# Attention with a gated convolution on one core: start addresses of the tiles that TensorE reads, and the layout of mirrored blocks

## The chip, the cores and the metric

The kernel runs on one core of a Trainium2 chip. The metric is the time of one execution on the device in microseconds (us); the median of several runs is given with the lowest and the highest.

## The reference

Eight batches of a sequence of 3200 with 256 channels. Attention weights are the squared positive part of the scaled products of z with itself, without a softmax; its result, times u, goes through a causal convolution of width 5 whose sigmoid gates a product with w_val, and a last product with w_out gives the output.

```python
scores = (1.0 / S) * np.matmul(z, z.transpose(0, 2, 1))    # z: (8, 3200, 64)
attn = np.maximum(scores, 0.0) ** 2
x = u * np.matmul(attn, v)                                  # u, v: (8, 3200, 256)
xp = np.concatenate([zeros((B, 4, D)), x], axis=1)
gate_pre = sum(conv_w[k] * xp[:, k:k + S, :] for k in range(5))
gate = 1.0 / (1.0 + np.exp(-gate_pre))
out = (gate * (x @ w_val)) @ w_out
```

## The kernel before

A batch's 3200 positions are 25 tiles of 128. As queries they are taken in seven chunks, four of 512 columns and then three of 384 (in the last batch five of 512, one of 384 and one of 256). As keys they are taken in 13 pairs of tiles, of which the last has one. A step is one chunk with one pair of key tiles; 8 x 7 x 13 = 728 steps follow one another in an order written out by hand.

All products are of float32 values cut into a high and a low part (type float32r), so one product is three on TensorE: low by high, high by low, high by high. In a step, `attend` or `attend_whole` multiplies the values of the key pair (`v_hl0` to `v_hl12`, the stationary operand, one tile for each pair) with the attention weights (`ah`, `al`, the moving operand, four buffers each) and adds them up in two PSUM banks (`acc0`, `acc1`): 2 key tiles x 3 parts x 2 halves of the channels = 12 products. The attention weights of the step three further on are made meanwhile: either from scores (z tiles `zhl0` to `zhl6`, one for each chunk, are stationary and moving operand; `scores`, then two activations on ACT, lines 399 and 400), or, since attention is symmetric, from a block that an earlier chunk has made, turned round on DVE (line 355) and kept in DRAM: a mirrored step. `weights_of` casts either kind to `ah` (line 402 on ACT, or 404 on DVE) and subtracts for `al` (line 405, DVE). A mirrored block comes from DRAM into `m` with the quarter a (32 keys of each tile) outermost and the key tile j inside it; `ah` and `al` have the same layout, and `attend_list` reads each key tile's part in four runs.

Two forms of step follow from this. Where the step three further on needs scores, whose products use 64 of the 128 rows, all products are issued as pairs of 64-row halves by `side_by_side` (line 292): 12 pairs for the values and 3 for the scores. This is a halved step. Where it is mirrored there are no scores, and `attend_whole` issues 12 products of 128 rows (line 440): a full step. From the second batch on, mirrored are 2, 4, 6, 8, 9 and 11 of the 13 steps in the second to seventh chunk.

Between the steps, a list with due times (`BEHIND`) lets the chunk before go through `gated` (times u, into `x`), the convolution on DVE (line 511), the sigmoid, `value` (with `w_val`, lines 292 and 548), `gate_value` (into `gv`, then `gvh` and `gvl`) and `project` (with `w_out`, moving operand; `gvh` and `gvl` stationary; lines 292 and 614).

SBUF tiles come from two pools. A tile with a tag of its own gets its own place, one behind the other in an order that the kernel's first uses give; tiles with a common tag and `bufs=1` share one. In the program's map of addresses, `cw_raw` (80 bytes for each partition, in a slot of 96) lies at 131264 and `x` (2 x 516 x 4 = 4128 bytes) at 217376; most other tiles have 2048, 3072 or 4096 bytes. The tiles that TensorE reads begin, modulo 512: the weights, `zhl0` to `zhl2`, `v_hl0` to `v_hl2`, `ah`, `al`, `xh`, `xl` at 192, all below 131072; `v_hl3` to `v_hl12`, `zhl3` to `zhl6` and `gvh` at 288, all above it; `gvl` at 320, also above. `cw_raw` is filled at step -1 (`fetch_conv`) and read until step 9 (`convert_conv`); `gv` is first written at step 19.

Of the kernel before, what the change touches and what calls it, by code (L numbers as in the profile page):

```python
# [7 lines left out]
F32 = mybir.dt.float32  # L8
F32R = mybir.dt.float32r
U32 = mybir.dt.uint32  # L10
AF = mybir.ActivationFunctionType
ALU = mybir.AluOpType
P = 128
BLK = 32
# [3 lines left out]
def attn_glu_kernel(  # L18
# [30 lines left out]
    KW = conv_w.shape[0]  # L49
    HALO = KW - 1  # L50
    NT = S // P
    DH = D // P
# [8 lines left out]
    i = even.index(base) if extra < n_chunks else None  # L61
# [5 lines left out]
    all_homes = [[(c, t) for c, n in enumerate(sz) for t in range(n)] for sz in all_sizes]  # L67
    CW = P * max(max(sz) for sz in all_sizes)

    const = ctx.enter_context(tc.tile_pool(name="const", bufs=1))  # L70
    sb = ctx.enter_context(tc.tile_pool(name="sb", bufs=2))
    ps = ctx.enter_context(tc.tile_pool(name="ps", bufs=2, space=bass.MemoryType.PSUM))
# [2 lines left out]
    def f32(ap):  # L75
        return ap.bitcast(F32)
# [42 lines left out]
    w_raw = {}  # L119

    def fetch_conv():
        w_raw["conv"] = sb.tile([P, DH, KW, 2], U32, name="cw_raw", bufs=1)
        for h in range(DH):
            nc.sync.dma_start(w_raw["conv"][:, h], conv_w[:, h * P : (h + 1) * P, :].rearrange("k p two -> p k two"))

# [210 lines left out]
    mirror, m_in, turned_, to_keep = {}, {}, {}, []  # L336

    def keeps(b, c):
        return b > 0 or c > 1

    def mirrored(b, c, i):
        return all(all_homes[b][t][0] < c and keeps(b, all_homes[b][t][0]) for t in range(pairs[i][0], sum(pairs[i])))

    def turn(b, c, i, a):

        w = all_sizes[b][c] * P
        if not keeps(b, c):
            return
        for j, g, t, m in runs(b, i):
            if g > c:  # L350
                size = all_sizes[b][g]
                if (b, c, g) not in turned_:
                    turned_[b, c, g] = sb.tile([P, 4 * CW], F32, name="turned", bufs=2)
                into = turned_[b, c, g][:, : w * size].rearrange("p (m t x) -> p t m x", t=size, x=BLK)
                nc.vector.transpose(  # L355
                    into[:, t : t + m], a[:, j * w : (j + m) * w].rearrange("p (t m x) -> p t m x", t=m, x=BLK)
                )
                if t + m == size:
                    to_keep.append((b, c, g))
# [22 lines left out]
    def cast_on_scalar(b, c, i):  # L382

        return mirrored(b, c, i) or (c == 0 and i > 2) or (c > 0 and (b == B - 1 or c < n_chunks - 1 or i < 4))

    def weights_of(b, c, i):

        k, n = pairs[i]
        w = all_sizes[b][c] * P
        ah = sb.tile([P, 2 * CW], F32R, name="ah", bufs=AHEAD + 1)  # L390
        al = sb.tile([P, 2 * CW], F32R, name="al", bufs=AHEAD + 1)
        hi, lo = ah[:, : n * w], al[:, : n * w]
        if mirrored(b, c, i):
            a = m_in.pop((b, c, i))[:, : n * w]
        else:
            s = st_.pop((b, c, i))
            a = sb.tile([P, 2 * CW], F32, name="a", bufs=2)[:, : n * w]
            each = n * w // 2
            nc.scalar.activation(a.rearrange("p (j x) -> p j x", j=2), s[:, :, :each], AF.Relu, scale=scale)  # L399
            nc.scalar.activation(a, a, AF.Square)  # L400
        if cast_on_scalar(b, c, i):
            nc.scalar.copy(hi, a)  # L402
        else:
            nc.vector.tensor_copy(hi, a)
        nc.vector.tensor_tensor(lo, a, f32(hi), op=ALU.subtract)  # L405
        if not mirrored(b, c, i):
            turn(b, c, i, a)
        at[b, c, i] = (ah, al)
# [4 lines left out]
    def attend_list(b, c, i, h, first=False, last=False):  # L413
        k, n = pairs[i]
        w = all_sizes[b][c] * P
        if (b, c) not in accs:
            accs[b, c] = [ps.tile([P, 512], F32, name=f"acc{x}", bufs=1) for x in range(DH)]
        ah, al = (x[:, : n * w] for x in at[b, c, i])
        if mirrored(b, c, i):
            ah, al = (x.rearrange("p (a j x) -> p j a x", a=P // BLK, j=n) for x in (ah, al))  # L420
        else:
            ah, al = (x.rearrange("p (j x) -> p j x", j=n) for x in (ah, al))
        vh, vl = vt[b, i][:, 0], vt[b, i][:, 1]
        acc = accs[b, c][h][:, :w]
        hs = slice(h * P, (h + 1) * P)
        out_ = []
        for j in range(n):
            for m, (vp, ap_) in enumerate(((vl, ah), (vh, al), (vh, ah))):
                out_.append((acc, vp[:, j, hs], ap_[:, j], first and j == m == 0, last and j == n - 1 and m == 2))
        return out_  # L430

    def attend(b, c, i, part):

        x = (i + part) % 2
        sides = (attend_list(b, c, i, h, part == 0 and i == 0, part == 1 and i == NP - 1) for h in (x, 1 - x))
        turn_round("acc", sides, part)

    def attend_whole(b, c, i, h):
        for out_, st, mv, first, last in attend_list(b, c, i, h, i == 0, i == NP - 1):
            nc.tensor.matmul(out_, st, mv, start=first, stop=last)  # L440
# [22 lines left out]
    xs, xhl, gates, gvs, pvs, pos = {}, {}, {}, {}, {}, {}  # L463

    def gated(b, c, h):
        w = all_sizes[b][c] * P
        if h == 0:
            xs[b, c] = sb.tile([P, DH, HALO + CW], F32, name="x", bufs=1)
        x = xs[b, c]
        nc.vector.tensor_tensor(  # L470
            x[:, h, HALO : HALO + w], accs[b, c][h][:, :w], ut[b, c][:, h, :w], op=ALU.mult
        )
        if h == 0:
            if c == 0:
                nc.gpsimd.memset(x[:, :, :HALO], 0.0)
            else:
                nc.gpsimd.tensor_copy(x[:, :, :HALO], halos.pop((b, c - 1)))
# [201 lines left out]
    for b in range(B):  # L679
# [34 lines left out]
        else:  # L714
# [14 lines left out]
            for load in loads:  # L729
                at_step(*load)  # L730
    at_step(-1, fetch_conv)
    at_step(4, fetch_weights, "val", w_val, "gvh")
    at_step(9, fetch_weights, "out", w_out, "ob")
# [4 lines left out]
    with tc.manual_schedule():  # L738
        for s in range(min(todo), N):
            b, c, i = steps[s] if s >= 0 else (0, 0, -1)  # L740
# [3 lines left out]
            if s <= END:  # L744
# [25 lines left out]
                if i == NP - 1:  # L770
                    for h in range(DH):
                        gated(b, c, h)
# [3 lines left out]
                if ahead:  # L776
                    weights_of(*ahead)
            elif s == END + 1:
                for h in range(DH):
                    for r in range(s, N):  # L780
                        attend_whole(*steps[r], h)
                    gated(b, c, h)
                    x_high(b, c, one[h])
                    x_low(b, c, one[h])
                    for k in range(KW):
                        conv(b, c, h, k)
                    sigmoid(b, c, one[h])
# [47 lines left out]
```

## Time and profile before

| | |
|---|---|
| median of 3 runs | 2372.27 us (2371.66 to 2373.46) |
| the profiled execution | 2374.35 us, its span 2372.6 us |
| TensorE products busy | 2349.4 us, 99% of the span, 18894 of them |
| TensorE weight loads busy | 2065.3 us, 87% |
| VectorE (DVE) busy | 1792.8 us, 76% |
| ScalarE (ACT) busy | 1776.0 us, 75% |

Busy is the time in which an engine has at least one instruction under way. Products of TensorE overlap: the next starts while the last columns of one drain, so a product's own duration is longer than its share of the time. In a stretch that TensorE fills without a gap, the elapsed time divided by the number of products is the distance from one start to the next. Stretches below begin where a step begins and end where one ends.

### The profile page before, as it was taken

How to read it: one execution, taken by the hardware profiler on the slowest of the kernel's cores; microseconds unless marked ns; L12 is line 12 of the kernel's file. 1: busy time of each engine (PE TensorE's matmuls, PEld its weight loads, DVE VectorE, ACT ScalarE, POOL GpSimd, SP SyncE). 2: the span in 40 equal slices, each digit the busy share in tenths (PEclk: the TensorE clock that was granted, in tenths of full speed). 3: DMA queues.
4: the chain of work that ended last, by engine and by line, in shares of the span. 5: the costliest groups of instructions: out<-in, count | busy, mean ns of one | idle time of the engine just before them, and what ended most of it. 6: DMA issues, size and time to landing. Idle time of an engine off the chain costs nothing.

```text
span 2372.6 us, 47211 instructions
## 1 busy us (share of the span) xinstructions
PE 2349.4 (99%) x18894; PEld 2065.3 (87%) x18894; DVE 1792.8 (76%) x2265; ACT 1776.0 (75%) x2313; POOL 33.6 (1%) x108
## 2 busy tenths in 40 slices
PE   8999999999999999999999999999999999999998
PEld 6898998889888899888988899888998889988888
DVE  7776777787777777778787787777877778677775
ACT  7888868777777767777688775887768876687764
POOL 0000000000000000000000000000000000000000
PEclk9999999999999999999999999999999999999999
DMA  6155597778977789667896778866897778966552
GB/s 128 37 141 138 147 237 182 206 189 212 244 185 198 186 224 242 179 185 197 238 227 165 192 213 233 213 180 178 230 231 190 181 200 236 250 144 156 162 170 76
DMA packets 660013, 446.12 MB, mean 188 GB/s; under 512 B 349008, under 2 KB 614480, under 8 KB 659792
## 3 DMA queue, kind: packets, MB, share of 16 engines
q1 hardware_dynamic: 658736, 442.97, 70.9%
q8 instruction: 148, 2.42, 0.4%
q14 instruction: 73, 0.60, 0.1%
q10 hardware_dynamic: 1056, 0.13, 0.0%
HBM read 240.92 MB, written 202.05 MB: 187 GB/s over the span
## 4 chain that ended last, share of the span: by engine, by line
PE 96%; ACT 2%; DVE 1%; DMA 1%; issue 0%; SPq 0%; ACTq 0%; DVEq 0%
PE acc L292 45%; PE acc L440 28%; PE s L292 11%; PE misc L292 6%; PE misc L614 4%; PE misc L548 1%; ACT a L400 0%; ACT a L399 0%; DMA z_raw<-in_z_dram 0%; ACT ah L402 0%; DMA u_raw<-in_u_dram 0%; DVE gate L511 0%; DVE al L405 0%; DMA m<-mir 0%; DVE x L470 0%
## 5 line engine op out<-in xcount | busy, mean ns | idle before, releaser
L292 PE MATMUL acc<-ah,v_hl 64*128 64x512 f32 (+1 forms) x6656 | 1114.7, 380 | 8.3 <-DVE x L470 3.5
L292 PEld LDWEIGHTS acc<-ah,v_hl 64*128 64x128 f32 x6656 | 663.4, 185 | 120.4 <-issue 14.5
L405 DVE TENSOR_TENSOR al<-a,ah 128x1024 fp32r<-128x1024 f32 (+3 forms) x429 | 472.2, 1101 | 380.5 <-ACT ah L402 375.4
L292 PE MATMUL acc<-al,v_hl 64*128 64x512 f32 (+1 forms) x3328 | 665.1, 378 | 0.0
L440 PE MATMUL acc<-ah,v_hl 128*128 128x384 f32 (+2 forms) x2272 | 644.2, 359 | 0.9 <-ACT ah L402 0.9
L399 ACT ACTIVATE a<-s 128x1024 f32<-128x1024 f32 (+3 forms) x429 | 397.1, 926 | 219.5 <-PE s L292 217.7
L440 PEld LDWEIGHTS acc<-ah,v_hl 128*128 128x128 f32 x2272 | 416.5, 188 | 50.8 <-issue 6.6
L400 ACT ACTIVATE a<-a 128x1024 f32<-128x1024 f32 (+3 forms) x429 | 413.4, 964 | 14.0
L440 PE MATMUL acc<-al,v_hl 128*128 128x384 f32 (+2 forms) x1136 | 404.9, 356 | 0.1
L405 DVE TENSOR_TENSOR al<-m,ah 128x768 fp32r<-128x768 f32 (+2 forms) x299 | 306.5, 1025 | 115.5 <-ACT ah L402 114.7
L402 ACT CAST ah<-a 128x1024 fp32r<-128x1024 f32 (+3 forms) x391 | 374.0, 957 | 12.7
L292 PEld LDWEIGHTS acc<-al,v_hl 64*128 64x128 f32 x3328 | 339.8, 185 | 46.2
L402 ACT CAST ah<-m 128x768 fp32r<-128x768 f32 (+2 forms) x299 | 262.5, 892 | 150.8 <-DMA m<-mir 106.3
L355 DVE STREAM_TRANSPOSE turned<-a 128x1024 f32<-128x1024 f32 (+3 forms) x314 | 314.9, 1010 | 1.8 <-DMA mir<-turned 1.7
L511 DVE SCALAR_TENSOR_TENSOR gate<-x,cw,gate 128x512 f32<-128x512 f32 (+2 forms) x448 | 304.8, 680 | 4.1
L292 PE MATMUL s<-zhl,zhl 64*128 64x512 f32 (+3 forms) x1950 | 275.3, 373 | 0.0
L440 PEld LDWEIGHTS acc<-al,v_hl 128*128 128x128 f32 x1136 | 213.7, 188 | 16.7 <-DVE al L405 0.3
L292 PEld LDWEIGHTS s<-zhl,zhl 64*128 64x128 f32 x1950 | 194.4, 186 | 29.5 <-ACT a L399 0.6
L564 ACT CAST gvh<-gv 128x512 fp32r<-128x512 f32 (+2 forms) x112 | 64.3, 574 | 58.1 <-DVE gv L560 58.1
L292 PE MATMUL s<-zhl 64*128 64x512 f32 (+3 forms) x624 | 91.3, 376 | 7.1 <-DVE zhl L203 7.1
L516 ACT ACTIVATE gate<-gate 128x512 f32<-128x512 f32 (+2 forms) x112 | 65.3, 583 | 39.2 <-DVE gate L511 39.2
L492 ACT CAST xh<-x 128x1024 fp32r<-128x1024 f32 (+2 forms) x57 | 53.7, 942 | 42.8 <-DVE x L470 42.7
(97 smaller groups left out, 1861.0 us busy)
## 6 DMA issues: line engine op xcount, KB each, us to landing
m<-mir SPq DMA_DIRECT2D x187, 384.0 KB, 5.0
mir<-turned SPq DMA_DIRECT2D x332, 192.0 KB, 3.9
mir<-turned SPq DMA_DIRECT2D x188, 256.0 KB, 4.1
m<-mir SPq DMA_DIRECT2D x94, 512.0 KB, 6.1
v_hl<-v_kept SPq DMA_DIRECT2D x84, 512.0 KB, 7.0
v_kept<-v_made SPq DMA_DIRECT2D x71, 512.0 KB, 4.0
u_raw<-in_u_dram SPq DMA_DIRECT2D x264, 64.0 KB, 3.3
out_dram<-ob SPq DMA_DIRECT2D x33, 512.0 KB, 4.1
```

Of the source, the lines that this page charges most:

```text
L292: ins = nc.tensor.matmul(out_, st[r], mv[r], start=first, stop=last)
L355: nc.vector.transpose(into[:, t : t + m], a[:, j * w : (j + m) * w].rearrange("p (t m x) -> p t m x", t=m, x=BLK))
L399: nc.scalar.activation(a.rearrange("p (j x) -> p j x", j=2), s[:, :, :each], AF.Relu, scale=scale)
L400: nc.scalar.activation(a, a, AF.Square)
L402: nc.scalar.copy(hi, a)
L405: nc.vector.tensor_tensor(lo, a, f32(hi), op=ALU.subtract)
L440: nc.tensor.matmul(out_, st, mv, start=first, stop=last)
L492: nc.scalar.copy(xhl[b, c][0][:, hs, :w], xs[b, c][:, hs, HALO : HALO + w])
L511: nc.vector.scalar_tensor_tensor(g, tap, cw[:, h, k : k + 1], g, op0=ALU.mult, op1=ALU.add)
L516: nc.scalar.activation(g, g, AF.Sigmoid)
L564: nc.scalar.copy(gvs[b, c][0][:, e, :w], gv_[b, c, e][:, :w])
L614: nc.tensor.matmul(out_, st, mv, start=first, stop=last)
```

## The change

One constant is added: `X_ROW`, the row of `x`, is 512 + 64 elements instead of 516, so `x` has 4608 bytes. `cw_raw` gets the tag of `gv`, so it takes that tile's place instead of one of its own. With these two, all tiles that TensorE reads begin at 192 modulo 512. In `weights_of`, a mirrored block is still read from `m` with the quarter outermost, but `ah` and `al` are written with the key tile outermost and the quarter inside it; `attend_list` then reads every block as it reads one that was made from scores.

```diff
@@ -67,6 +67,9 @@
     CW = P * max(max(sz) for sz in all_sizes)
 
+    X_ROW = CW + P // 2
+    assert HALO <= P // 2
+
     const = ctx.enter_context(tc.tile_pool(name="const", bufs=1))
@@ -119,7 +122,7 @@
     def fetch_conv():
-        w_raw["conv"] = sb.tile([P, DH, KW, 2], U32, name="cw_raw", bufs=1)
+        w_raw["conv"] = sb.tile([P, DH, KW, 2], U32, name="cw_raw", tag="gv", bufs=1)
         for h in range(DH):
@@ -391,7 +394,8 @@
         hi, lo = ah[:, : n * w], al[:, : n * w]
         if mirrored(b, c, i):
-            a = m_in.pop((b, c, i))[:, : n * w]
+            a = m_in.pop((b, c, i))[:, : n * w].rearrange("p (a j x) -> p a j x", a=P // BLK, j=n)
+            hi, lo = (x.rearrange("p (j a x) -> p a j x", a=P // BLK, j=n) for x in (hi, lo))
         else:
@@ -416,10 +420,7 @@
         ah, al = (x[:, : n * w] for x in at[b, c, i])
-        if mirrored(b, c, i):
-            ah, al = (x.rearrange("p (a j x) -> p j a x", a=P // BLK, j=n) for x in (ah, al))
-        else:
-            ah, al = (x.rearrange("p (j x) -> p j x", j=n) for x in (ah, al))
+        ah, al = (x.rearrange("p (j x) -> p j x", j=n) for x in (ah, al))
@@ -465,7 +466,7 @@
         if h == 0:
-            xs[b, c] = sb.tile([P, DH, HALO + CW], F32, name="x", bufs=1)
+            xs[b, c] = sb.tile([P, DH, X_ROW], F32, name="x", bufs=1)
         x = xs[b, c]
```

## Rows read from the trace of the kernel before

**Rows 1.** The page: TensorE's busy time, and its granted clock in 40 slices.

```profile
PE 2349.4 (99%) x18894; PEld 2065.3 (87%) x18894; DVE 1792.8 (76%) x2265; ACT 1776.0 (75%) x2313; POOL 33.6 (1%) x108
...
PEclk9999999999999999999999999999999999999999
```

**Rows 2.** The page: the chain that ended last, shares of the span by engine.

```profile
PE 96%; ACT 2%; DVE 1%; DMA 1%; issue 0%; SPq 0%; ACTq 0%; DVEq 0%
```

**Rows 3.** TensorE's waits, costliest first: us in total, times, longest us.

```profile
PE s L292 <- DVE zhl L203: 7.1, 1, 7.1
PE acc L292 <- DVE x L470: 3.5, 2, 3.2
```

**Rows 4.** TensorE's products by shape: count, busy us, mean ns, idle us.

```profile
L292 PE MATMUL acc<-ah,v_hl 64*128 64x512 f32 x4936 | 866.5, 394 | 8.1 <-DVE x L470 3.5 <-DVE v_hl L250 2.6 <-ACT a L400 1.7
L292 PE MATMUL acc<-al,v_hl 64*128 64x512 f32 x2468 | 518.5, 394 | 0.0
L440 PE MATMUL acc<-ah,v_hl 128*128 128x384 f32 x1356 | 357.5, 340 | 0.0
L440 PE MATMUL acc<-ah,v_hl 128*128 128x512 f32 x832 | 270.9, 398 | 0.0
...
L440 PE MATMUL acc<-al,v_hl 128*128 128x512 f32 x416 | 164.0, 394 | 0.0
...
L614 PE MATMUL misc<-w_out_hi,gvl 128*128 128x256 f32 x260 | 74.1, 285 | 0.0
```

**Rows 5.** Windows, full steps of v_hl11, v_hl1 (512 columns): us, PE, PEld, clock, DMA.

```profile
1043.65:1046.46 2.81, 2.81 (x13) 2.26 (x12) 1.00 1.05 343
1053.44:1056.16 2.72, 2.72 (x13) 2.25 (x12) 1.00 1.16 269
```

**Rows 6.** Windows, halved steps: second chunk's v_hl2, v_hl3, v_hl4; fourth chunk's v_hl7.

```profile
963.26:966.71 3.45, 3.45 (x32) 1.00 0.01 2
966.71:970.23 3.52, 3.52 (x33) 1.00 0.75 173
970.23:973.75 3.52, 3.52 (x32) 1.00 0.21 41
1075.85:1079.36 3.51, 3.51 (x32) 1.00 0.18 74
```

**Rows 7.** Windows, 384 columns: full (runs, one run), value; halved (runs, one run).

```profile
1096.09:1104.55 8.46, 8.46 (x48) 8.46 (x49) 1.00 0.86 226
1124.93:1128.05 3.12, 3.12 (x19) 2.96 (x18) 1.00 0.93 286
...
1177.15:1179.24 2.09, 2.09 (x12) 1.93 (x12) 1.00 0.98 305
...
1114.94:1117.60 2.66, 2.66 (x32) 1.00 0.87 201
1117.60:1120.22 2.62, 2.62 (x32) 1.00 0.46 70
```

**Rows 8.** Windows, 256 columns: v_hl1 and v_hl2, v_hl3 and v_hl4; 24 projections.

```profile
2336.69:2339.57 2.88, 2.88 (x26) 2.88 (x25) 1.00 0.31 91
2339.57:2342.39 2.82, 2.82 (x26) 2.82 (x25) 1.00 0.86 284
...
1047.87:1050.70 2.83, 2.83 (x24) 2.79 (x23) 1.00 1.04 339
```

**Rows 9.** DVE by shape: count, busy us, mean ns, idle us and what ended it.

```profile
L405 DVE TENSOR_TENSOR al<-a,ah 128x1024 fp32r<-128x1024 f32 x302 | 369.8, 1225 | 266.5 <-ACT ah L402 261.9 <-PE s L292 2.4
L355 DVE STREAM_TRANSPOSE turned<-a 128x1024 f32<-128x1024 f32 x177 | 219.1, 1238 | 0.8 <-DMA mir<-turned 0.7
```

**Rows 10.** Windows, the fourth batch's fifth, sixth, seventh chunk: us, DVE busy, clock, DMA.

```profile
1096.09:1130.90 34.81, 27.16 (x37) 1.00 0.77 206
1130.90:1164.40 33.50, 24.37 (x38) 1.00 0.78 200
1164.40:1199.18 34.78, 26.89 (x41) 1.00 1.06 270
```

## The prediction

> **What bounds the kernel now.** I read the busy shares first, then the chain of work that ended last, then TensorE's waits, then TensorE's products by shape, and last the elapsed time of single steps. The reader is to see that TensorE is the only thing that counts: it is busy 99% of the span with its clock granted in full, that is at 2.4 GHz, in every slice [rows 1]; the chain runs through it for 96% [rows 2]; of its waits the costliest comes to 7.1 us in the whole span and the next to 3.5 us [rows 3]. So the time is the number of products times the distance from the start of one to the start of the next. That distance is what I look for, and not the mean duration, which holds the drain behind the last column as well.
>
> The distance is not a constant. A step takes the 12 products of one pair of key tiles (v_hl0 to v_hl12). At line 440, where a product uses all 128 rows, a step of v_hl11 with 512 columns takes 2.81 us, 234 ns for each product; a step of v_hl1, with the same shape, takes 2.72 us, 227 ns [rows 5]. Since 512 columns at 2.4 GHz are 213 ns, the bare overhead falls from 21 to 14 ns. In the steps where products run as pairs of 64-row halves beside the scores (line 292), 15 pairs with 512 columns take 3.45 us with v_hl2 and 3.52 us with v_hl3 and v_hl4 [rows 6]. The break lies between v_hl2 and v_hl3, and all later tiles are like v_hl3. In the program's map of addresses that is where cw_raw lies: 80 bytes in a slot of 96. Ahead of it every tile that TensorE reads begins at 192 modulo 512 (the weights, zhl0 to zhl2, v_hl0 to v_hl2, ah, al, xh, xl); behind it at 288 (v_hl3 to v_hl12, zhl3 to zhl6, gvh); gvl, behind x with its 4128 bytes, at 320. So it is the steps whose stationary tile and moving tile begin at different residues that are slow. A hint that the two count together: in the fourth chunk the scores read moving and stationary from tiles at 288, and there a halved step takes 3.51 us, with the key products still mixed [rows 6].
>
> A second loss is in mirrored steps, where the moving operand is read in four runs. With 384 columns, four full steps in runs take 8.46 us for 48 products, 176.3 ns each; one and a half steps read in one run take 3.12 us for 18, 173.3 ns [rows 7]. The first are of v_hl0 to v_hl3, on both sides of the break, the second of tiles at 288; twelve value products with weights at 192 and one run take 2.09 us, 174 ns [rows 7]. So at 384 columns it is the runs that cost and not the residue. Halved, a step of 2.66 us becomes one of 2.62 us [rows 7].
>
> **The change part by part.** Products are counted in the order of the program; the sum of the shapes is in [rows 4].
>
> 1. cw_raw shares gv's buffer and x grows to 4608 bytes, nine times 512. All other tiles there are multiples of 512 bytes, so everything TensorE reads comes to 192, the state that v_hl0 to v_hl2 have today.
>  - Full steps, 512 columns: 852 of the 1248 products of line 440 take a stationary tile at 288, which is 71 steps. 71 x (2.81 - 2.72) = 6.4 us saved.
>  - Halved steps, 512 columns: 5820 of the 7404 products take one at 288, which is 242.5 steps. Some 50 of them have scores from zhl3 and go from 3.51 to 3.45, the other 192 from 3.52 to 3.45: 50 x 0.06 + 192 x 0.07 = 16.4 us. The scores' own gain is in these steps. Least: 0.06 for all, 14.6 us. Most: if pairs come down to the 227 ns that a full product reaches, 15 x 0.227 = 3.40 us and 242 x 0.12 = 29 us. I take 3.45, for it is measured on the very form.
>  - 384 columns: nothing, by the 173.3 and 174 ns of [rows 7]. The value products of lines 292 and 548 read tiles at 192 already: nothing.
>  - 256 columns: here equal residues look worse. In the last chunk two steps with v_hl1 and v_hl2 take 2.88 us (120 ns), two with v_hl3 and v_hl4 2.82 us (117.5 ns) [rows 8]. The projection of line 614 now runs at 2.83/24 = 117.9 ns [rows 8]; if it goes to 120, its 780 products and the 276 pairs of line 292 lose 1056 x 2.1 = 2.2 us. The other end is nothing, since projection reads its weights as moving operand, which that row does not show. I take the loss.
>  - Other work: cw_raw is filled at step -1 and last read at step 9; gv is first written at step 19, so no wait arises. x, gv and halo are read by DVE, ACT and POOL alone; POOL's copies into x touch the same few columns.
>
> 2. Mirrored blocks are written by key tile, so their products read one run. With 384 columns 1536 full products are 128 steps: 128 x (8.46/4 - 3.12/1.5) = 128 x 0.035 = 4.5 us. 1584 halved ones are 66 steps: 66 x 0.04 = 2.6 us. With 512 columns runs cost nothing: the step of v_hl1 in [rows 5] is a mirrored one. The price is on ACT and DVE, whose cast (line 402) and subtraction (line 405) now put down 128 or 96 elements at a time instead of 1024 or 768 in one. The nearest row is DVE's transpose (line 355), which writes runs of 32 elements: 1238 ns against 1225 for a plain subtraction of the size [rows 9]. I take nothing to 13 ns for each of 299 blocks, and it is covered: in the fifth to seventh chunk of a batch DVE works 27.16 of 34.81, 24.37 of 33.50 and 26.89 of 34.78 us [rows 10]. No DMA, wait or queue is moved.
>
> Sum: 6.4 + 16.4 - 2.2 + 4.5 + 2.6 = 27.7 us. A faster TensorE asks more of ACT and DVE by 1%, which the same windows leave room for. The profiled execution took 2374.35 us (span 2372.6, 1.75 around it), the median of the runs is 2372.27; 2374.35 - 27.7 = 2346.7 and, from the median, 2344.6. I forecast 2345. With the bounds (14.6 or 29 for the halved steps, 0 or 2.2 for the 256 columns, runs at half or all) the forecast's own range is 2333 to 2350.
>
> **A rule against it.** The rows show that a tile's residue and a moving operand's runs go with 3 to 7 ns of a product [rows 5, 7]. The Trainium skill's page "SBUF — State Buffer", section Specifications (TRN2), gives lines of 16 bytes and full bandwidth from two hits on one; 192, 288 and 320 and runs of 384 bytes are all multiples of 16, so by it neither edit would change anything. Its page "TensorE: Matmul & The Clock Gate", Part 2, says that loading the next weights takes no read bandwidth from the running product, by which a stationary tile's place could not lengthen one. The trace differs by the 7 ns above, if these belong to the place and not to the step.
>
> **The rivals.**
> A: the residue is not what counts. v_hl0 to v_hl2 also lie below address 131072 and v_hl3 to v_hl12 above it, and ah and al below; the trace can't part this from the residue. Then the tiles stay where they are in that sense, and only part 2 remains: 2372.3 - 7.1 = 2365. Against it stands little: the fourth chunk's scores, both operands above, are no slower, so lying above is not slow in itself [rows 6]. Chance 0.12.
> B: the differences belong to the steps (what else runs in the first three of a chunk), and neither place nor runs matter: 2372. Against it: the break falls between v_hl2 and v_hl3 in chunks with quite different neighbours [rows 5, 6]. The 16-byte rule named above would end here. Chance 0.06.
> C, slower: writing in pieces is dear on DVE, and DVE becomes the bound of the late chunks. It has 7.65, 9.13 and 7.89 us free there [rows 10] for 8, 9 and 11 mirrored blocks. Up to some 1.0 us more for each, a doubling, the 27.7 us are not used up; at 1.2 us more the chunks run over by 2.0, 1.7 and 5.3 us, 9 us in each of seven batches, and 2345 + 63 = 2408. Against it stand the 13 ns of the transpose. Chance 0.04.
>
> **How the numbers follow.** Forecast 0.78, A 0.12, B 0.06, C 0.04. About 0.2% (4.7 us) is what a measurement here can tell from no change. Faster by more than that: all of the forecast and two thirds of A, 0.86; same: the rest of A and B, 0.10; slower 0.04. The range reaches from the forecast's lower end to A's time with a little room, 2333 to 2367, and leaves out B, C and what I have not thought of.
>
> **What will show it.** If part 1 is right, full steps of v_hl10 and v_hl11 take 2.72 us and halved steps 3.45 us whatever their tile; if A holds, they stay at 2.81 and 3.52. If part 2 is right, full mirrored steps of the fifth chunk take 2.08 us. The projection of 24 products tells by 2.83 or 2.88 us whether 256 columns lose. For C, lines 402 and 405 would show it in their means. I am wrong in size if halved steps fall below 3.40 us, and in kind if a step of v_hl11 doesn't move.

## The result, and the profile after the change

| | before | after |
|---|---|---|
| median (lowest to highest) | 2372.27 us (2371.66 to 2374.03), 5 runs | 2350.34 us (2346.95 to 2352.55), 5 runs |
| ratio to before, 95% interval | 1 | 0.9904 (0.989 to 0.9919) |
| the profiled execution, its span | 2374.35 us, 2372.6 us | 2350.68 us, 2348.9 us |

The kernel is 1.0% faster, 21.9 us by the medians and 23.7 us by the two profiled executions. The forecast was 2345 us with a range of 2333 to 2367. The direction and the mechanism came as forecast; the gain was put 4 us too high by the profiled executions and 5 to 6 us by the medians.

The page of the kernel after shows nearly the same shares as [rows 1]: TensorE is as full as before, its clock is granted in full (a 9 is 90% or more) in every slice, and it is busy for 23.6 us less.

```profile
PE 2325.8 (99%) x18894; PEld 2047.1 (87%) x18894; DVE 1790.1 (76%) x2265; ACT 1774.0 (76%) x2313; POOL 34.2 (1%) x108
...
PEclk9999999999999999999999999999999999999999
```

The next fence has windows of the trace after. A line gives the stretch, its length in us, TensorE's busy time with the number of products under way in it, in some lines the same for weight loads, then the granted clock, the share of DMA and GB/s. They are, in order, full steps with 512 columns of v_hl11, v_hl1 and v_hl10; a halved step of v_hl4 in the second chunk; halved steps with 384 columns in the fifth chunk, v_hl7, which is mirrored, and v_hl8, which is not; full steps with 384 columns of v_hl1 and v_hl10; and the 24 projections between the third and the fourth chunk.

```profile
1032.80:1035.52 2.72, 2.72 (x14) 2.25 (x13) 1.00 1.04 331
1042.50:1045.22 2.72, 2.72 (x14) 2.25 (x13) 1.00 1.09 334
1074.81:1077.68 2.87, 2.87 (x12) 2.36 (x13) 1.00 0.97 310
...
960.35:963.81 3.46, 3.46 (x32) 1.00 0.22 41
1103.31:1105.94 2.63, 2.63 (x32) 1.00 1.13 237
1105.94:1108.57 2.63, 2.63 (x32) 1.00 0.60 155
...
1086.72:1088.80 2.08, 2.08 (x13) 2.08 (x13) 1.00 0.71 115
1111.11:1113.33 2.22, 2.22 (x13) 2.22 (x13) 1.00 0.95 228
...
1036.88:1039.75 2.87, 2.87 (x26) 1.00 1.03 343
```

The step of v_hl11 went from 2.81 us [rows 5] to 2.72, what v_hl1 had and kept; the halved step from 3.52 [rows 6] to 3.46; the full mirrored step with 384 columns from 2.115 (a quarter of the 8.46 of [rows 7]) to 2.08; the halved mirrored v_hl7 from 2.66 to 2.63 and v_hl8 from 2.62 to 2.63 [rows 7]; the projection from 2.83 [rows 8] to 2.87. Two rows did not do as told: v_hl10 with 512 columns, for which the prediction had 2.72 us, only went from 2.91 to 2.87, and with 384 columns it became slower, from 2.18 to 2.22. The rows of before for these two:

```profile
1086.13:1089.04 2.91, 2.91 (x14) 1.00 0.95 324
1122.75:1124.93 2.18, 2.18 (x14) 1.00 0.95 231
```

ACT and DVE did not feel the writing in pieces. In the groups by shape of the trace after, the casts of mirrored blocks at line 406 and the subtractions at line 409 (402 and 405 before, with means of 832, 1047, 949 and 1222 ns there) have the means they had:

```profile
L406 ACT CAST ah<-m 128x768 fp32r<-128x768 f32 x194 | 159.1, 833 | 58.2 <-DMA m<-mir 36.2 <-PE acc L441 16.4 <-ACT ob L631 4.4
L406 ACT CAST ah<-m 128x1024 fp32r<-128x1024 f32 x94 | 96.7, 1049 | 80.4 <-DMA m<-mir 72.0 <-PE acc L441 8.2
...
L409 DVE TENSOR_TENSOR al<-m,ah 128x768 fp32r<-128x768 f32 x194 | 183.8, 947 | 40.6 <-ACT ah L406 39.6
L409 DVE TENSOR_TENSOR al<-m,ah 128x1024 fp32r<-128x1024 f32 x94 | 114.8, 1221 | 73.7 <-ACT ah L406 73.7
```

### The profile page after: what moved, and what is told of

Its sections match the earlier page's. It is cut to its first block, busy times and chain, and to the rows that moved or that the text cites. A ratio compares the mean times of both kernels' runs of the same rounds, so it can differ in the third digit from the quotient of the medians.

```text
span 2348.9 us, 47211 instructions
## 1 busy us (share of the span) xinstructions
PE 2325.8 (99%) x18894; PEld 2047.1 (87%) x18894; DVE 1790.1 (76%) x2265; ACT 1774.0 (76%) x2313; POOL 34.2 (1%) x108
## 4 chain that ended last, share of the span: by engine, by line
PE 94%; ACT 2%; DVE 1%; DMA 1%; issue 1%; SPq 0%; ACTq 0%; DVEq 0%
PE acc L295 44%; PE acc L441 28%; PE s L295 11%; PE misc L295 6%; PE misc L615 4%; PE misc L549 1%; ACT a L404 1%; ACT a L403 1%; DMA u_raw<-in_u_dram 1%; ACT ah L406 1%; DMA v_raw<-in_v_dram 0%; DMA z_raw<-in_z_dram 0%; DVE al L409 0%; DVE x L471 0%; DVE gate L512 0%
## 5 line engine op out<-in xcount | busy, mean ns | idle before, releaser
L295 PE MATMUL acc<-ah,v_hl 64*128 64x512 f32 (+1 forms) x6656 | 1103.3, 377 | 7.0 <-DVE v_hl L253 2.6
L295 PEld LDWEIGHTS acc<-ah,v_hl 64*128 64x128 f32 x6656 | 656.3, 185 | 118.6 <-issue 13.3
L295 PE MATMUL acc<-al,v_hl 64*128 64x512 f32 (+1 forms) x3328 | 658.3, 376 | 0.0
L441 PE MATMUL acc<-ah,v_hl 128*128 128x384 f32 (+2 forms) x2272 | 637.8, 356 | 0.8 <-ACT ah L406 0.8
```

The lines of the kernel that those rows point to most:

```text
L295: ins = nc.tensor.matmul(out_, st[r], mv[r], start=first, stop=last)
```

## The experiments

Each kernel is told as a diff or in words; lines left out of a diff are marked by three dots. Fences hold windows as above, all from the fourth batch. From the third to the seventh batch a step takes the same time in each batch to 10 ns, so steps can be compared to that accuracy, while the time of a run scatters by 2 us and more. In what follows the distance is the start of the stationary tile less the start of the moving one, in bytes, modulo 512.

### One part at a time

The addresses alone (e1), in the kernel before, with the constant `X_ROW` added as in the change:

```diff
-        w_raw["conv"] = sb.tile([P, DH, KW, 2], U32, name="cw_raw", bufs=1)
+        w_raw["conv"] = sb.tile([P, DH, KW, 2], U32, name="cw_raw", tag="gv", bufs=1)
...
-            xs[b, c] = sb.tile([P, DH, HALO + CW], F32, name="x", bufs=1)
+            xs[b, c] = sb.tile([P, DH, X_ROW], F32, name="x", bufs=1)
```

> Addresses alone: cw_raw in gv's place, x with 4608 bytes, mirrored blocks laid out as before. If the two parts add up, the steps with 512 columns take what they take after the change (full v_hl11 2.72 us, halved 3.46 us) and mirrored steps with 384 columns what they took before (2.11 us full, 2.66 us halved): 2350.3 + 6.3 = 2357 us. The 6.3 us are the difference of the steps with 384 columns between the two traces (4.2 full, 2.1 halved). If the runs cost only while the tiles are apart, 2350 us.

Measured: 2353.47 us, ratio 0.9921 (0.9904 to 0.9937). Windows: full v_hl11 and halved v_hl4 with 512 columns; full v_hl1 and halved v_hl7, both mirrored, with 384.

```profile
1032.97:1035.69 2.72, 2.72 (x13) 1.00 1.07 357
960.53:963.99 3.46, 3.46 (x34) 1.00 0.20 38
1086.93:1089.04 2.11, 2.11 (x13) 1.00 0.87 119
1103.66:1106.31 2.65, 2.65 (x32) 1.00 0.83 200
```

The steps with 512 columns have all of their gain, those with 384 remain in runs at 2.11. The time is 3.5 us lower than the expectation's sum, which took the whole difference of the two traces in these steps for the layout's. 1.3 us of it are a wait at the start of the second batch, of which more below. From the third to the seventh batch each one is 0.5 to 0.7 us slower than after the change, but the first two are no slower in sum, since their waits differ from trace to trace.

The layout alone (e2), in the kernel before: the edits in `weights_of` and `attend_list`, with cw_raw and x as they were.

> The layout of mirrored blocks alone: cw_raw and x as before. If the parts add up: mirrored steps with 384 columns at 2.08 us, steps with 512 columns as before (full v_hl11 2.81 us, halved 3.52 us): 2372.3 - 6.3 = 2366 us. If the layout is worth nothing by itself, 2372 us; if casts that write in pieces cost ACT or DVE something, lines 402 and 405 have other means than 1047 and 1222 ns.

Measured: 2366.25 us, ratio 0.9976 (0.9967 to 0.9985). Windows: the same four steps, and the halved v_hl8, which is not mirrored.

```profile
1040.45:1043.26 2.81, 2.81 (x13) 1.00 1.03 331
967.02:970.55 3.53, 3.53 (x32) 1.00 0.21 40
1094.97:1097.05 2.08, 2.08 (x13) 1.00 0.82 110
1111.54:1114.16 2.62, 2.62 (x32) 1.00 0.73 188
1114.16:1116.78 2.62, 2.62 (x32) 1.00 0.89 200
```

This is rival A's time, 2365, and the layout's share is as the prediction had it, with 2.08 and 2.62 us. But the halved steps take 2.62 us here, where tiles are 96 bytes apart, and 2.63 after the change, where they are not. So at 384 columns equal starts cost something in halved steps; one run gives a mirrored one 0.04 us at 96 bytes (2.66 [rows 7] to 2.62) and only 0.01 to 0.02 with equal starts (2.65 in e1 to 2.63 after); and the two parts don't quite add up: they gain 18.9 and 6.1 us alone, 25.0 in sum, and 21.9 together, with a scatter of the runs of 2 us.

### Is it the distance of the two starts, or the place of one?

Moving operands elsewhere (e8): in the kernel after, `v_made`, with the raw tile that shares its place, gets 96 bytes more and cw_raw a slot of 416 bytes. ah, al, v_hl1, v_hl2 and zhl2 then begin at 288, all else at 192.

```diff
-        w_raw["conv"] = sb.tile([P, DH, KW, 2], U32, name="cw_raw", tag="gv", bufs=1)
+        cw_raw = sb.tile([P, 104], U32, name="cw_raw", bufs=1)
+        w_raw["conv"] = cw_raw[:, : DH * KW * 2].rearrange("p (h k two) -> p h k two", h=DH, two=2)
...
-        v_made[b, g, t] = sb.tile([P, 2, 2, D], F32R, name="v_made", bufs=1)
+        v_made[b, g, t] = sb.tile([P, 4 * D + 24], F32R, name="v_made", bufs=1)[:, : 4 * D].rearrange("p (x t d) -> p x t d", x=2, t=2)
```

> As after the change, but ah, al, v_hl1, v_hl2 and zhl2 begin at 288 modulo 512, everything else that TensorE reads at 192. Theory (the distance counts): steps of v_hl1 and v_hl2 stay at 2.72 us with both operands at 288, steps of v_hl0 and v_hl3 to v_hl12, whose stationary tile is still at 192, go to 2.81 us full and 3.5 halved; time about 2365 us. Rival (the stationary tile's own residue counts, 192 fast and 288 slow): v_hl11 stays at 2.72 us, v_hl1 goes to 2.81, time about 2355 us.

Measured: 2373.93 us, ratio 1.0009 (1.0 to 1.0019). Windows: full steps of v_hl11, v_hl1 and v_hl2, then the halved v_hl4, all with 512 columns; full steps of v_hl3 and v_hl11 with 384.

```profile
1040.08:1042.88 2.80, 2.80 (x14) 1.00 1.01 334
1049.93:1052.70 2.77, 2.77 (x14) 1.00 1.11 275
1052.70:1055.51 2.81, 2.81 (x14) 1.00 0.78 147
966.52:970.02 3.50, 3.50 (x33) 1.00 0.19 39
...
1098.92:1101.04 2.12, 2.12 (x13) 1.00 1.06 393
1121.52:1123.64 2.12, 2.12 (x14) 1.00 0.79 238
```

v_hl11 lies where it is fast after the change, at 192, and is slow, because ah and al have moved away: the stationary tile's own place decides nothing. v_hl2 takes 2.81 us as it does before and after the change in this place, where the first halved products follow on it. v_hl1, with equal starts, takes 2.77 and not the 2.72 expected: it comes behind the slow v_hl0, and in the trace its products start 235 ns apart at first and 227 at the end, as those of v_hl10 do after the change. The whole is no faster than before and 9 us slower than the theory's 2365. The theory's figures are those of a distance of +96. At -96 one key pair more has unequal starts, and full steps with 384 columns take 2.12 us, where they take 2.08 at +96 (v_hl3 and v_hl11 in e2). So a distance of -96 undoes all that the two parts gain, and at 384 columns its sign counts.

All tiles elsewhere (e3): in the kernel after, the constant tile `cw` is made 96 bytes larger, so that everything behind it begins at 288.

```diff
-        cw = const.tile([P, DH, KW], F32, name="cw")
+        cw = const.tile([P, 40], F32, name="cw")[:, : DH * KW].rearrange("p (h k) -> p h k", k=KW)
```

> As after the change, but all tiles that TensorE reads begin at 288 modulo 512. Theory (the distance of the two starts counts, not where they lie): the same steps as after the change, 2.72 us for v_hl11 and 3.46 halved, 2350 us. Rival (192, or a start on a line of 64 bytes, is the good place): 2.80 us and more, 2365 us.

Measured: 2350.17 us, ratio 0.9909 (0.9892 to 0.9925); v_hl11, halved v_hl4, halved v_hl8 with 384 columns:

```profile
1034.54:1037.26 2.72, 2.72 (x13) 1.00 1.02 342
962.10:965.56 3.46, 3.46 (x33) 1.00 0.18 35
1107.69:1110.32 2.63, 2.63 (x32) 1.00 0.65 105
```

The steps are those of the kernel after. 192 is no better place than 288, and a start on a multiple of 64 bytes is not what counts; what the steps of e2, e3 and e8 with 512 columns go with is the distance.

### Which distances?

Four kernels differ from the kernel after in cw_raw's slot alone, n bytes (576, 544, 128, 256). The tiles behind it, v_hl3 to v_hl12, zhl3 to zhl6, gvh and gvl, then begin 64, 32, 128 and 256 bytes further than the others, modulo 512.

```diff
-        w_raw["conv"] = sb.tile([P, DH, KW, 2], U32, name="cw_raw", tag="gv", bufs=1)
+        cw_raw = sb.tile([P, n // 4], U32, name="cw_raw", bufs=1)
+        w_raw["conv"] = cw_raw[:, : DH * KW * 2].rearrange("p (h k two) -> p h k two", h=DH, two=2)
```

> As after the change, but v_hl3 to v_hl12, zhl3 to zhl6, gvh and gvl begin at 256 modulo 512, 64 bytes from the other tiles. Theory (the distance of stationary and moving start modulo 512 counts): full steps of v_hl11 at 2.81 us, halved at 3.5, time 2366 us, what the layout alone gives. Rival (what counts is that a tile begins on a line of 64 bytes, which 288 does not): 2.72, 3.46 and 2350 us.

> As after the change, but the later tiles begin 32 bytes further, at 224 modulo 512. If any distance costs, v_hl11 takes 2.80 us and the time is 2364 us, as 64 bytes apart; if the loss grows with the distance (64: 2.80, 96: 2.815), 2.75 to 2.79 us and some 2357 us.

> As after the change, but the later tiles begin 128 bytes further, at 320. If the loss grows with the distance, v_hl11 at 2.82 us or more and 2366 us; if the period is 128 bytes, 2.72 and 2350.

> As after the change, but the later tiles begin 256 bytes further, at 448. If the period is 256 bytes, v_hl11 at 2.72 us and 2350 us; if it is 512, half the period apart, 2.8 us and about 2365, or less than that if the loss has its peak near 96 bytes on either side.

| distance | median us, ratio (95% interval) | v_hl11, full | v_hl4, halved | v_hl8, halved, 384 columns |
|---|---|---|---|---|
| 0 (after) | 2350.34, 0.9904 (0.989 to 0.9919) | 2.72 | 3.46 | 2.63 |
| 32 | 2363.81, 0.9968 (0.9957 to 0.9979) | 2.80 | 3.52 | 2.61 |
| 64 | 2364.26, 0.9964 (0.9951 to 0.9977) | 2.80 | 3.50 | 2.64 |
| 96 (e2) | 2366.25, 0.9976 (0.9967 to 0.9985) | 2.81 | 3.53 | 2.62 |
| 128 | 2364.90, 0.9971 (0.9962 to 0.998) | 2.80 | 3.49 | 2.66 |
| 256 | 2348.75, 0.9905 (0.989 to 0.992) | 2.72 | 3.46 | 2.63 |

The windows of the kernel with 32 bytes, then of the one with 256, for the three steps of the table:

```profile
1037.23:1040.03 2.80, 2.80 (x13) 1.00 1.03 333
963.83:967.35 3.52, 3.52 (x33) 1.00 0.20 39
1110.86:1113.47 2.61, 2.61 (x32) 1.00 0.69 108
```

```profile
1031.01:1033.73 2.72, 2.72 (x14) 1.00 1.10 346
958.56:962.02 3.46, 3.46 (x32) 1.00 0.21 39
1104.15:1106.78 2.63, 2.63 (x32) 1.00 0.83 126
```

At 512 columns each distance from 32 to 128 bytes costs about the same, 0.08 to 0.09 us for a full step and 0.03 to 0.07 for a halved one; the expectation that the loss grows with the distance fell. 256 bytes are as good as none, and the -96 of e8, which is 160 modulo 256, is slow. So a period of 256 bytes fits all of them, and the 512 of the change were more than needed: its tiles would also do at 192 and 448. The rival of the lines of 64 bytes fell with the kernel at 64 (2.80 us), that of a period of 128 bytes with the one at 128.

At 384 columns the distance alone does not decide. With 64 bytes, full steps of v_hl3 and v_hl11 take, in this order:

```profile
1094.64:1096.76 2.12, 2.12 (x13) 1.00 1.05 396
1117.14:1119.22 2.08, 2.08 (x13) 1.00 0.92 264
```

### A version by width of the product

The prediction had put down that 256 columns are slower with equal starts, and e2 and e5 show the same of halved steps with 384. So the starts were set apart where the products are narrow, first for the projection (e9), by moving gvh's and gvl's data 64 bytes on. Their buffers are 512 bytes larger, and so is the raw weight that shares gvh's.

```diff
-                sb.tile([P, DH, CW], F32R, name="gvh", bufs=1),
-                sb.tile([P, DH, CW], F32R, name="gvl", bufs=1),
+                sb.tile([P, DH * CW + 128], F32R, name="gvh", bufs=1)[:, 16 : 16 + DH * CW].rearrange("p (h w) -> p h w", h=DH),
+                sb.tile([P, DH * CW + 128], F32R, name="gvl", bufs=1)[:, 16 : 16 + DH * CW].rearrange("p (h w) -> p h w", h=DH),
```

> As after the change, but the data of gvh and gvl begin 64 bytes further, at 256 modulo 512, while w_out stays at 192. Theory (products of 256 columns are slower where both operands start at one residue): the 24 projections of a chunk with 512 columns go back from 2.87 to 2.83 us or a little less, some 2 us over the kernel, 2348 us; no other step changes. Rival (the projection became slower for another reason, such as x's place): 2.87 and 2350 us.

Measured: 2348.79 us, ratio 0.9904 (0.9887 to 0.992). The 24 projections between third and fourth chunk:

```profile
1036.06:1038.89 2.83, 2.83 (x26) 1.00 0.89 267
```

They are back at 2.83 us with no other tile moved modulo 512, so it was the equal starts that had made them slower. The median is 1.5 us lower than that of the kernel after, but the kernel before was 1.8 us faster too in this round of runs (2370.5 us), and the ratio is the same: in the whole time no gain is shown.

Then the attention weights of the narrow chunks as well (e10): e9 with

```diff
+        o = 56 if w < CW else 0
-        hi, lo = ah[:, : n * w], al[:, : n * w]
+        hi, lo = ah[:, o : o + n * w], al[:, o : o + n * w]
...
-        at[b, c, i] = (ah, al)
+        at[b, c, i] = (ah[:, o : o + n * w], al[:, o : o + n * w])
```

> As e9, and in chunks narrower than 512 columns ah and al are written 224 bytes further into their buffers, so the stationary tile begins 32 bytes behind the moving one modulo 256. Theory: the distance that costs at 512 columns is worth something at 384: halved steps 2.633 to 2.613 us, the first full step of v_hl10 2.216 to 2.19, other full steps 2.08 as they are; 2 us less than e9, 2346 us. Rival (384 columns are best with equal starts, and what e2 showed came from elsewhere): 2348 us, halved steps at 2.633.

Measured: 2346.3 us (2345.74 to 2346.46), ratio 0.9894 (0.9879 to 0.9908). Halved v_hl8 and full v_hl10 with 384 columns; v_hl11 with 512:

```profile
1103.68:1106.30 2.62, 2.62 (x34) 1.00 0.69 114
1108.82:1111.01 2.19, 2.19 (x15) 1.00 0.99 232
...
1030.71:1033.43 2.72, 2.72 (x13) 1.00 1.05 342
```

The narrow steps fall as told (halved ones from 2.63 to 2.62, v_hl10 from 2.22 to 2.19), the wide ones stay. Against e9, measured in the same round, the median is 2.5 us lower. This is the fastest kernel of the study by its median. Of the 4 us to the changed one a part is the faster round; by the ratios it is 0.1%, some 2.4 us, and the two intervals overlap.

## Why the prediction was right, and where its sum was off

The time lies in the range and the likeliest case came true. It lies at the upper end of what the forecast's own bounds gave, though (2350.34 us against 2333 to 2350); the given range was wider because it reached to rival A's time. The lower end of 2333 doesn't come out of its bounds either: with 29 us for the halved steps and no loss at 256 columns the sum is 42.5 us, which gives 2330 to 2332. **The bound** was read rightly: nearly all that changed in the span is the distance between TensorE's products, and no wait took its place.

**Part 1.** That the steps of v_hl1 and v_hl2 show what later ones would take is right to 10 ns for v_hl11 and the halved v_hl4; the steps for which it is not follow below. Rival A, the half of the memory, fell with the result itself: v_hl11 lies above address 131072 as before and takes 2.72 us. Rival B, the step, fell with the same row, and with e8, where the slow steps move along with the distance. The two rules of the Trainium skill that the prediction set against the change would have given no gain. One is the Trainium skill's page "SBUF — State Buffer", section Specifications (TRN2), with lines of 16 bytes: distances of 32, 64 and 128 bytes are all multiples of 16, and each costs 0.08 us on 2.72. The other is the Trainium skill's page "TensorE: Matmul & The Clock Gate", Part 2, by which loading the next weights takes no read bandwidth from the running product. What the stationary tile's place does here, 0.08 us on 2.72 for 32 bytes (e5), raises a doubt whether that holds for these operands, but the runs don't show whether it is the two reads that meet.

**Part 2** is right in its mechanism: one run saves a full step what was forecast, but a halved one, once its starts are equal, less than half of it. The price that it put on ACT and DVE, nothing to 13 ns a block, came at its lower end: the means of casts and subtractions moved by 2 ns at most, so rival C fell.

The sum was 27.7 us, and 23.7 us came between the two profiled executions. Adding up, in both traces, the distance from each product's start to the next by class gives the terms, in us:

| term | forecast | measured |
|---|---|---|
| full steps, 512 columns | -6.4 | -4.8 |
| halved steps, 512 columns, with their scores | -16.4 | -14.3 |
| full steps, 384 columns | -4.5 | -4.2 |
| halved steps, 384 columns | -2.6 | -0.2 |
| projection, 256 columns | +2.2 | +1.5 |

Two smaller terms were not in the forecast: the scores with 384 columns, -0.5 us, and the wait for `x` behind a projection at the start of the second batch (the second of [rows 3]), -1.3 us; it differs between runs. Of the projection's 1.5 us only 1.0 are the equal starts, in the products of 128 rows. The halved ones, for which the forecast had 0.6 us, lost nothing by them: their part is a wait in the first batch that grew by 0.7 us.

Three steps of the working were mis-sized. First, "384 columns: nothing" was read from full steps alone. Halved ones lose with equal starts nearly what one run gives them: by the same sums one run gives 2.0 us (e2 against before), and equal starts take 1.8 us back (after against e2; 2.62 us a step at a distance of 96, 2.63 at none, in all halved steps and not only in mirrored ones). The prediction had the rows that show a loss at 256 columns and did not look for one in halved steps at 384. Second, "71 steps" priced all full steps at v_hl11's gain of 0.09 us, but a step of v_hl10, the first full one behind halved ones, gains only 0.03 to 0.04. The trace after shows why. In this stretch v_hl10 begins at 1074.81; the fence has the start of each row, its length, and the products merged into it:

```profile
1074.81 0.50 PE L441 MATMUL acc<-ah,v_hl 128*128 128x512 f32 x1
1075.14 0.40 PE L441 MATMUL acc<-al,v_hl 128*128 128x512 f32 x1
1075.38 0.63 PE L441 MATMUL acc<-ah,v_hl 128*128 128x512 f32 x2
1075.85 0.39 PE L441 MATMUL acc<-al,v_hl 128*128 128x512 f32 x1
1076.07 0.63 PE L441 MATMUL acc<-ah,v_hl 128*128 128x512 f32 x2
1076.54 0.39 PE L441 MATMUL acc<-al,v_hl 128*128 128x512 f32 x1
1076.77 0.62 PE L441 MATMUL acc<-ah,v_hl 128*128 128x512 f32 x2
1077.23 0.39 PE L441 MATMUL acc<-al,v_hl 128*128 128x512 f32 x1
1077.45 0.62 PE L441 MATMUL acc<-ah,v_hl 128*128 128x512 f32 x2
1077.91 0.39 PE L441 MATMUL acc<-al,v_hl 128*128 128x512 f32 x1
1078.13 0.62 PE L441 MATMUL acc<-ah,v_hl 128*128 128x512 f32 x2
1078.59 0.39 PE L441 MATMUL acc<-al,v_hl 128*128 128x512 f32 x1
```

The first distance, 0.33 us, is the passage from pairs to full products and is the same before the change (0.34). Then, from one al product to the next are three products: 0.71, 0.69, 0.69, 0.68 and 0.68 us, the last of them in the step that follows. They come down to 227 ns each only at the end of the step, having begun near 236. Third, the halved step ended at 3.46 and not at 3.45, and the steps that hold the value products (v_hl5) gained half as much, 0.03 us (6.22 to 6.19 in the second chunk). That is 2 us; the term came out at 14.3, a little under its lower bound of 14.6.

## What to carry to other kernels

Where TensorE is the bound, measure the distance between the starts of products of one form, tile by tile: two values for one form can point to where operands lie, and a stray tile of 80 bytes in the pool can be the cause. Lay out buffers so that stationary and moving operand begin at one residue modulo 256 bytes for float32r products of 512 columns, but price it apart for each width: at 384 and 256 columns some distances were better. A sum priced from one representative step should be checked on a step at a transition and on every width before its terms are multiplied.

## What the runs showed of the hardware

- With float32r operands, a product of 128 rows and 512 columns follows the one before after 227 ns where the starts of stationary and moving tile are equal modulo 256 bytes (0 and 256 apart), and after 233 to 235 ns where they are 32, 64, 96, -96 or 128 bytes apart (2.80 to 2.81 us for 12). Other distances were not tried at this width. Where the pair lies as a whole (192 or 288 modulo 512) makes no difference.
- The width counts, and at 384 columns the sign. There 32 and 96 bytes apart leave a full step at 2.08 us, and -96 makes it 2.12 (e8); with 64 bytes between them a step of v_hl3 takes 2.12 and one of v_hl11 2.08, so it is not the distance alone; with 128, v_hl11 takes 2.11. At 256 columns it is turned round: 2.88 us for 24 equal, 2.82 apart [rows 8].
- The rate settles: with equal starts and 512 columns, the first full step behind products of 64 rows (v_hl10), or behind a step with unequal starts (v_hl1 in e8), needs about ten products until they follow at 227 ns.
- Runs of 96 elements in the moving operand cost a full product 3 ns (2.11 against 2.08 us for 12 in e1), runs of 128 nothing (v_hl1 takes 2.72 us before and after). Why that is so, and what in the array or the memory the period of 256 bytes belongs to, these runs do not show.
